# Moving the joined PVs by one round and the score steps by one to six in chunk 0 of a fused attention and SwiGLU block

## The chip, the cores and the metric

The kernel runs on one core of a Trainium2 chip. The metric is the device time of one execution in microseconds (us), the median of several runs. Before the change it is 559.22 us (three runs, 559.13 to 559.57).

## The reference

The block normalises `x` (2048 rows of 576), and adds to `x` a sliding-window attention (32 heads of 18 channels, a window of 256 keys) and a gated SwiGLU network (4608 hidden channels), both of the normalised rows:

```python
xn = layernorm(x)
q, k, v = split_heads(xn @ wqkv)                  # 32 heads, 18 channels
mask = (i - j >= 0) & (i - j < 256)
p = softmax(where(mask, q @ k.T * 18**-0.5, -1e9))
a = (p @ v) @ wo
h = silu(xn @ w1) * (xn @ w3)
out = x + a + h @ w2
```

## The kernel before

The 2048 rows are done in four chunks of 512 (`c` = 0 to 3). A chunk has three stages on TensorE:

- Projections (L449): q, k and v of the chunk's rows. In chunk 0 they stand ahead of everything, with the layer norm.
- Gate and up (`unit_pairs`, L701): 36 **units** `u` of 128 hidden channels. A unit is nine **rounds** `n` = 0 to 8; a round is two matmuls of 64 rows each, one in either half of the array, that run side by side, one into the up bank and one into the gate bank. Behind a unit ScalarE computes a tanh of the gate bank (`unit_tanh`, L710), and VectorE makes `gs` (L716, reads the gate bank) and `hT` (L719, reads the up bank).
- The second product (`p2_list`, L761) with `w2`, 288 matmuls a chunk, and the product with `wo` (L767, L687).

Attention is woven into the gate/up stage of its chunk. Its heads are in eight groups `g` of four; a group has four **score steps** `s` in chunk 0 (32 in all) and five in later chunks (40). A step (g, s) is: scores on TensorE (`scores`, L575), into the two banks kept for them (`SC`, banks 6 and 7), an exp on ScalarE that reads both (`exps`, L584), and masks on POOL (`masks`, L611). The next step's scores must wait until the exp has read the banks. A **PV** `j` (`pv`, L632) multiplies the weights of groups 2j and 2j+1 with v; VectorE takes the result out by two transposes (`pv_out`, L641), then come a reciprocal, a scaling on POOL (`o_scale`, L647), turning (`o_turn`, L654) and DMAs to `oT`. PV 0 stands behind a unit; PVs 1 and 2 stand together, **the joint**, at unit and round `JOINT[c]`; PV 3 stands at the end of gate/up.

PSUM has eight banks. Six make three pairs that are handed out in turn (`job()`): each unit takes a pair, and PV 0 takes one between two units. At the joint, unit u is half done and holds a pair; PV 1 takes the pair of unit u-2 and PV 2 that of unit u-1, so PV 2 must wait until `hT` of unit u-1 is made. The next unit then takes PV 1's pair (so it waits for both of its transposes), and the one behind it PV 2's.

All engines' instructions are written in one order by hand; each engine runs its own in that order, and waits on semaphores are worked out from the buffers (`_Prog`). Where steps stand is set by a planner that counts a clock in rounds: a step may be placed ahead of a round once `clock >= nxt`, a step counts as one round, and

```python
soon = clock + 7.5
room = last - clock - PV_COST * (3 - next_pv) - 5 * sum(v > at_u for v in xt)
nxt = max(soon, clock + room / max(1, len(att) - done))
```

with `last = total - AHEAD[c]`: a smaller `AHEAD` spreads the chunk's steps further towards its end. Steps are at least 7.5 rounds apart, the step itself counted. Ahead of the rounds of a later chunk, steps are also placed among its projections. Weight loads (L322, L349) are issued by SP; some wait for a named round of TensorE.

Of the kernel before, what the change touches and what calls it, by code (L numbers as in the profile page):

```python
# [164 lines left out]
def bass_parallel_sum__sliding_block__glu_gated_swiglu__prompt_kernel(  # L165
# [32 lines left out]
    with ExitStack() as es:  # L198
# [34 lines left out]
        def pt_slot(sl):  # L233
            kind, n = sl
            if kind == "pt":
                return pt[:, n, :, :]
            if kind == "w2":
                return w2[n][:, :, :].rearrange("p f d -> p (f d)")[:, 0:2 * CH].rearrange("p (q r) -> p q r", r=2)
            if kind == "od":
                return od[n][:, :, :].rearrange("p g c -> p (g c)").rearrange("p (q r) -> p q r", r=2)  # L240
            if kind == "sh":
                two = stage[:, 2 * n:2 * n + 2, :]
            else:
                two = hT[:, NF - 8 + 2 * n:NF - 6 + 2 * n, :]
            return two.rearrange("p t c -> p (t c)").rearrange("p (q r) -> p q r", r=2)

        def pt_keys(sl):
            kind, n = sl
            if kind in ("pt", "w2", "od"):
                return [(kind, n)]  # L250
            if kind == "sh":
                return [("sh", 2 * n), ("sh", 2 * n + 1)]
            return [("h", NF - 8 + 2 * n), ("h", NF - 7 + 2 * n)]
# [21 lines left out]
        def job():  # L275
            nonlocal job_ctr
            i = job_ctr % 3
            job_ctr += 1
            return JOBS[i]
# [54 lines left out]
        def owe_part(op):  # L334
            nonlocal owed
            if owed:
                owed -= 1
                load_part((op,))
# [275 lines left out]
        def pv(c, j, banks):  # L614

            seen = set()
            n_all = sum(len(st) for st in steps_of(c))
            n = 0
            for s, st in enumerate(steps_of(c)):
                col = 0  # L620
                for kb, q0, nb in st:
                    n += 1
                    pos = (c * NB + kb) % NV
                    for gi in range(2):
                        g = 2 * j + gi
                        sl = pt_of[(c, g, s)]
                        for pr in range(2):
                            for p in range(2):
                                first = (p, gi, pr) not in seen
                                seen.add((p, gi, pr))  # L630
                                q = 2 * gi + pr
                                add("pe", lambda e, p=p, q=q, pr=pr, sl=sl, g=g, pos=pos, q0=q0, nb=nb, col=col, first=first, n=n: e.matmul(  # L632
                                    PS[32 * q:32 * q + VW, banks[p], q0 * KB:(q0 + nb) * KB],
                                    va[64 * p:64 * p + 64, pos, g, pr, :],
                                    pt_slot(sl)[64 * p:64 * p + 64, col * KB:(col + nb) * KB, pr],
                                    start=first, stop=(n == n_all), tile_position=(64 * p, 32 * q), skip_group_check=True),
                                    r=pt_keys(sl) + [("va", pos)], **{"j" if any(k[0] == p for k in seen - {(p, gi, pr)}) or not first else "w": [("ps", banks[p])]})
                    col += nb

        def pv_out(b, i):  # L640
            add("dve", lambda e, to=uqs[i]: e.transpose(to, PS[:, b, :]), r=[("ps", b)], w=uq_keys[i])  # L641

        def o_scale(i):
            u3 = uqs[i].rearrange("p (n d) -> p n d", d=32)
            o3 = oq[:, :].rearrange("p (n d) -> p n d", d=32)[:, :, 0:Dh]
            add("dve", lambda e: e.reciprocal(rden[:], u3[:, :, Dh]), r=uq_keys[i], w=["rden"])
            add("pool", lambda e: e.tensor_tensor(  # L647
                o3, u3[:, :, 0:Dh], rden[:].unsqueeze(2).to_broadcast([128, CH // 32, Dh]), ALU.mult),
                r=uq_keys[i] + ["rden", "oq0"], w=["oq"])
# [260 lines left out]
        span_main(2, G, "act", slice(0, 2))  # L910

        PV_COST, PV_AFTER = 6.6, 20
        JOINT = {0: (26, 5), 1: (27, 7), 2: (24, 4), 3: (27, 8)}
        AHEAD = [50, 24, 40, 24]

        for c in range(NC):
            NS = len(steps_of(c))
            att = [(g, s) for g in range(G) for s in range(NS)]
            near = {t: tuple(JOINT[c][0] - 13 + 4 * t + k for k in (0, 2, 3)) for t in range(3)} | {3: (34, 35, 40)}
            plan = near if c + 1 < NC else {}  # L920
# [7 lines left out]
            start = 60 if c == 0 else 42  # L928
            last = total - AHEAD[c]
            nxt = soon = start  # L930
            clock = 0.0
            done = 0
            pv_ready = {}
            free = [("pt", n) for n in range(NPT)]
            if c:
                free += [("sh", n) for n in range(4)]
            held = {6 * NS + 1: free.pop(), 6 * NS: free.pop()}
            early = [("h", n) for n in range(4)] + [("w2", (c * 2 * NFC + n) % NW2) for n in range(NW2)]
# [6 lines left out]
            def later(u, what):  # L945
                side.setdefault(u, []).append(what)

            def release(j, kept):
                for g in (2 * j, 2 * j + 1):
                    for st in range(NS):  # L950
                        sl = pt_of[(c, g, st)]
                        ok = ("pt", "sh", "h", "w2") if j == 0 else ("pt", "sh")
                        if sl[0] in ok:
                            (kept if kept is not None and len(kept) < 2 and sl[0] in ("pt", "sh") else free).append(sl)
# [45 lines left out]
            for u in range(NF):  # L1000
# [7 lines left out]
                for n in range(9):  # L1008
                    into = nxt - (clock + 9 - n)
                    if (u, n) == JOINT[c]:  # L1010
                        ja = 1
                        assert next_pv == ja and ja + 1 in pv_ready and clock >= pv_ready[ja + 1], (c, next_pv, clock, pv_ready)
                        two = [job(), job()]
                        job_ctr += 1
                        kept = []
                        _DEBUG.setdefault("joint", []).append((c, u, n, done, round(clock - pv_ready[ja + 1], 1), len([o for o in P.ops if o.eng == "pe"])))
                        for m, j in enumerate((ja, ja + 1)):
                            pv(c, j, two[m])
                            clock += PV_COST
                            release(j, kept)  # L1020
                        next_pv = ja + 2
                        for m, sl in enumerate(kept):
                            uqs[2 + m:] = [pt_slot(sl).rearrange("p q r -> p (q r)").bitcast(dt.float32)]
                            uq_keys[2 + m:] = [pt_keys(sl)]
                        pv_out(two[0][0], 0)
                        pv_out(two[0][1], 1)
                        o_scale(0)
                        pv_out(two[1][0], 2)
                        pv_out(two[1][1], 3)
                        g = 2 * ja  # L1030
                        later(u, lambda g=g: (o_turn(g, 0), o_turn(g, 1), o_scale(1)))
                        later(u + 1, lambda g=g: o_turn(g + 1, 0))
                        later(u + 2, lambda g=g, ja=ja: (o_turn(g + 1, 1), o_pack(ja, "sp"), o_scale(2)))
                        later(u + 3, lambda g=g: (o_turn(g + 2, 0), o_turn(g + 2, 1), o_scale(3)))
                        later(u + 3, lambda kept=kept: free.extend(kept))
                        later(u + 4, lambda g=g: o_turn(g + 3, 0))
                        later(u + 5, lambda g=g, ja=ja: (o_turn(g + 3, 1), o_pack(ja + 1, "sp")))
                    if done < len(att) and (free or done < len(early) or done in held) and (clock >= nxt or (n == 8 and into < 3 and clock >= soon)):
                        spaced_step()
                    op = unit_pairs(c, u, n, n + 1, b0[0])  # L1040
                    clock += 1
                    if n in (3, 8) or (n == 6 and c == 0 and u < 4):
                        owe_part(op)
# [41 lines left out]
                if c == 0 and u == 22:  # L1085
# [3 lines left out]
                    for r in range(2):  # L1089
                        add("sp", lambda e, r=r: e.dma_start(  # L1090
                            wo[64 * r:64 * r + 64, 4, :], head.rearrange("(t d) f -> t d f", d=Dh)[:, 0:16, :]), j=["wo"], dma="wo")
                if u in (range(26, 30) if c == 0 else range(JOINT[c][0], JOINT[c][0] + 7, 2)):
                    load_w2(c * 2 * NFC + 4)
# [68 lines left out]
```

## Time and profile before

| what | value |
|---|---|
| median of three runs | 559.22 us (559.13 to 559.57) |
| the profiled execution | 559.3 us, span 557.6 us |
| TensorE busy | 552.7 us, 99% of the span, 6766 matmuls |
| VectorE, ScalarE, POOL busy | 309.5, 259.5, 163.1 us |
| gate/up (L701), both sources | 183.7 + 151.6 us for the two largest groups |
| second product (L761) | 146.6 us, 1152 matmuls of 286 ns |
| scores (L575) | 51.5 us, 528 matmuls |
| exps (L584), mean by form | about 1010 ns, 1024 wide or a little less |
| tanh, gs, hT, mean | 594, 679, 687 ns |
| mean DMA rate | 154 GB/s |

The span is from the first to the last instruction of the profiled execution; 1.7 us of its time lie outside. In the groups, each matmul has the duration from its start to the modelled end of its pipeline, so two that run side by side or behind each other overlap, and the sum of durations is more than the busy time. A wait is shown as idle time of an engine before an instruction with what released it; gaps of TensorE under 0.15 us are not listed as waits, so a short delay is found from the distance between starts. In the timeline, `[0.34 <-DVE hT L719]` means that the engine was idle for 0.34 us until the instruction of line 719 on VectorE had ended.

The stages by time: opening and projections of chunk 0 to 21.75 us, gate/up of chunk 0 to about 103.2, its second product to 142.9; then chunk 1 to 280.3, chunk 2 to 417.6, chunk 3 to the end.

### The profile page before, as it was taken

The page shows a single profiled execution, that of the slowest core. Times are in us where ns is not written, and L with a number is a line of the kernel's source. Part 1 is how long each engine was busy: PE and PEld are TensorE (multiplying, and loading weights), DVE is VectorE, ACT ScalarE, POOL GpSimd, SP SyncE. Part 2 cuts the span into 40 slices and gives each one's busy share as a digit, 9 for nine tenths or more (in the row PEclk, how much of TensorE's full clock was granted, in tenths as well). Part 3 has the DMA queues.
Part 4 walks back from the last instruction along what each step waited for, and adds up shares of the span by engine and source line. Part 5 has one row for each costly group of instructions (what it writes and reads, how often), then busy time and mean ns, then how long its engine had stood idle before and what let it go on. Part 6 is the DMA issues. An engine that isn't in the chain of part 4 may idle for free.

```text
span 557.6 us, 15733 instructions
## 1 busy us (share of the span) xinstructions
PE 552.7 (99%) x6766; PEld 333.5 (60%) x6766; DVE 309.5 (56%) x578; ACT 259.5 (47%) x357; POOL 163.1 (29%) x389
## 2 busy tenths in 40 slices
PE   8999999999999999999999999999999999999998
PEld 4445454677655445477765544547776554455776
DVE  6476978610356877851045687874105577678211
ACT  6457766100287775700038777640005767755000
POOL 5513644300033452530003445423001333433000
PEclk9999999999999999999999999999999999999999
DMA  9987996877366379566726639685572673734552
GB/s 238 216 167 181 207 186 157 171 197 185 95 139 144 105 177 192 146 168 180 195 65 139 161 106 210 137 201 139 151 187 55 138 173 96 176 107 128 139 149 65
DMA packets 127072, 85.96 MB, mean 154 GB/s; under 512 B 34179, under 2 KB 124763, under 8 KB 127003
## 3 DMA queue, kind: packets, MB, share of 16 engines
q1 hardware_dynamic: 125011, 82.69, 63.0%
q10 hardware_dynamic: 1992, 2.27, 1.8%
q8 instruction: 53, 0.87, 0.7%
q14 instruction: 16, 0.13, 0.1%
HBM read 71.29 MB, written 2.36 MB: 132 GB/s over the span
## 4 chain that ended last, share of the span: by engine, by line
PE 97%; DVE 1%; DMA 1%; ACT 0%; issue 0%; POOL 0%
PE ps L701 50%; PE ps L761 25%; PE ps L449 9%; PE ps L575 6%; PE ps L632 3%; PE ps L767 3%; DMA xp<-in_A_x_dram 1%; PE ps L687 0%; PE ps L394 0%; DVE xn L374 0%; ACT stage L829 0%; ACT xnT L401 0%; DVE hT L719 0%; DVE gs L716 0%; ACT th L710 0%
## 5 line engine op out<-in xcount | busy, mean ns | idle before, releaser
L701 PE MATMUL ps<-xnT,w 64*128 64x512 bf16 x1400 | 183.7, 376 | 0.0
L701 PE MATMUL ps<-xnS,w 64*128 64x512 bf16 x1120 | 151.6, 376 | 0.0
L761 PE MATMUL ps<-w,hT 128*128 128x288 bf16 x1152 | 146.6, 286 | 0.0
L716 DVE SCALAR_TENSOR_TENSOR gs<-th,ps 128x512 bf16<-128x512 bf16 x144 | 97.7, 679 | 78.9 <-ACT th L710 78.5
L761 PEld LDWEIGHTS ps<-w,hT 128*128 128x128 bf16 x1152 | 112.3, 98 | 28.9 <-issue 0.4
L701 PEld LDWEIGHTS ps<-xnT,w 64*128 64x128 bf16 x1400 | 67.1, 94 | 65.7 <-DVE hT L719 0.3
L710 ACT ACTIVATE th<-ps 128x512 bf16<-128x512 f32 x144 | 85.5, 594 | 39.2 <-PE ps L701 37.2
L719 DVE SCALAR_TENSOR_TENSOR hT<-gs,ps 128x512 bf16<-128x512 bf16 x144 | 98.9, 687 | 4.9
L584 ACT ACTIVATE pt<-ps 128x1024 bf16<-128x1024 f32 (+1 forms) x70 | 70.7, 1011 | 39.6 <-PE ps L575 39.5
L701 PEld LDWEIGHTS ps<-xnS,w 64*128 64x128 bf16 x1120 | 53.5, 94 | 51.4
L774 DVE TENSOR_TENSOR ofin<-ps,xp 128x288 bf16<-128x288 f32 x32 | 13.8, 455 | 125.1 <-PE ps L767 67.0
L462 ACT ACTIVATE stage<-ps 128x512 bf16<-128x512 f32 x16 | 9.5, 596 | 142.2 <-PE ps L449 139.8
L611 POOL TENSOR_TENSOR hT<-hT,mk 128x128 int32<-128x128 int32 (+1 forms) x59 | 24.1, 429 | 173.8 <-ACT hT L584 173.7
L611 POOL TENSOR_TENSOR pt<-pt,mk 128x128 int32<-128x128 int32 (+1 forms) x124 | 50.1, 428 | 29.3 <-ACT pt L584 29.1
L575 PE MATMUL ps<-qv,kv 64*128 64x320 bf16 (+4 forms) x528 | 51.5, 260 | 0.0
L575 PEld LDWEIGHTS ps<-qv,kv 64*128 64x128 bf16 x528 | 25.6, 94 | 28.4 <-ACT hT L584 2.3
L449 PE MATMUL ps<-xnT,wp 64*128 64x512 bf16 (+1 forms) x360 | 37.9, 355 | 0.0
L584 ACT ACTIVATE w<-ps 128x1024 bf16<-128x1024 f32 (+1 forms) x32 | 32.3, 1010 | 11.3 <-PE ps L575 11.2
L584 ACT ACTIVATE hT<-ps 128x1024 bf16<-128x1024 f32 (+1 forms) x32 | 32.3, 1009 | 6.6 <-PE ps L575 6.2
L611 POOL TENSOR_TENSOR w<-w,mk 128x128 int32<-128x128 int32 (+1 forms) x56 | 22.8, 427 | 28.2 <-ACT w L584 28.2
L654 DVE STREAM_TRANSPOSE od<-oq 128x256 bf16<-128x256 bf16 x64 | 25.8, 428 | 6.9 <-POOL oq L647 6.9
L449 PEld LDWEIGHTS ps<-xnT,wp 64*128 64x128 bf16 x360 | 18.8, 94 | 14.5 <-POOL wp L885 0.2
(86 smaller groups left out, 380.6 us busy)
## 6 DMA issues: line engine op xcount, KB each, us to landing
w<-in_B_w_dram SPq DMA_DIRECT2D x208, 192.0 KB, 4.0
w<-in_B_w_dram SPq DMA_DIRECT2D x72, 288.0 KB, 3.3
xp<-in_A_x_dram SPq DMA_DIRECT2D x30, 144.0 KB, 3.4
out_dram<-ofin SPq DMA_DIRECT2D x32, 72.0 KB, 1.7
xnS<-xnT SPq DMA_DIRECT2D x8, 256.0 KB, 4.2
oT<-od SPq DMA_DIRECT2D x40, 36.0 KB
pt<-in_A_wqkv_dram SPq DMA_DIRECT2D x4, 288.0 KB, 6.7
hT<-in_B_w_dram SPq DMA_DIRECT2D x6, 192.0 KB, 3.6
```

What stands on the lines that cost most here:

```text
L449: op = add("pe", lambda e, out_=out_, st=st, mv=mv, n=n, r0=r0, first=first: e.matmul(out_, st, mv, start=first, stop=(part == 1 and n == ...
L575: add("pe", lambda e, r0=r0, out_=out_, kb=kb, q0=q0, nb=nb: e.matmul(out_, kb4[r0:r0 + 64, g, kb + NV - NB, :] if kb < 0 else kv[r0:r0 + ...
L584: add("act", lambda e: e.activation(pt_slot(sl)[:, 0:w, :], PS[:, SC[0]:SC[1] + 1, 0:w].rearrange("p r q -> p q r"), ACT.Exp, scale=scale) ...
L611: add("pool", lambda e, vb=vb, mm=mm: e.tensor_tensor(vb, vb, mm, ALU.mult), r=(key if n == 0 else []) + ["mk"], **{"w" if n == 0 else "j" ...
L632: add("pe", lambda e, p=p, q=q, pr=pr, sl=sl, g=g, pos=pos, q0=q0, nb=nb, col=col, first=first, n=n: e.matmul(PS[32 * q:32 * q + VW, banks ...
L654: add("dve", lambda e: e.transpose(od[i][:, g % 2, c0:c0 + CH // 2], oq[:, c0:c0 + CH // 2]), r=["oq", "oq0"], **{"j" if half or g % 2 els ...
L701: op = add("pe", lambda e, n=n, r0=r0, r=r, k=k, src=src: e.matmul(PS[:, b0 + r, :], wt[r0:r0 + 64, k, fl * 128:(fl + 1) * 128], src, star ...
L710: add("act", lambda e: e.activation(th[i][:], PS[:, bg, :], ACT.Tanh, scale=0.5), r=[("ps", bg)], w=[("th", i)])
L716: add("dve", lambda e: e.scalar_tensor_tensor(out=gs[i][:], in0=th[i][:], scalar=1.0, in1=PS[:, bg, :], op0=ALU.add, op1=ALU.mult), r=[("t ...
L719: add("dve", lambda e: e.scalar_tensor_tensor(out=hT[:, u, :], in0=gs[i][:], scalar=0.5, in1=PS[:, bu, :], op0=ALU.mult, op1=ALU.mult), r= ...
L761: add("pe", lambda e: e.matmul(bank, hT[:, f, tt * 128:(tt + 1) * 128], w2[sl][:, k, :], start=(f == 0 and half == 1), stop=False), r=[("h ...
L767: add("pe", lambda e: e.matmul(bank, oT[:, k, tt * 128:(tt + 1) * 128], wo[:, k, d0:d0 + HD], start=False, stop=(k == 3 and (half == 0 or ...
```

## The change

Three lines change. The joint of chunk 0 goes from round 5 to round 6 of unit 26 (the joint is placed ahead of the round). `AHEAD` of chunk 0 goes from 50 to 40. And no step may be placed ahead of round 0 of unit 0 in chunks 1 to 3.

```diff
-        JOINT = {0: (26, 5), 1: (27, 7), 2: (24, 4), 3: (27, 8)}
-        AHEAD = [50, 24, 40, 24]
+        JOINT = {0: (26, 6), 1: (27, 7), 2: (24, 4), 3: (27, 8)}
+        AHEAD = [40, 24, 40, 24]
...
-                    if done < len(att) and (free or done < len(early) or done in held) and (clock >= nxt or (n == 8 and into < 3 and clock >= soon)):
+                    if (c == 0 or u or n) and done < len(att) and (free or done < len(early) or done in held) and (clock >= nxt or (n == 8 and into < 3 and clock >= soon)):
                         spaced_step()
```

What the planner makes of it in chunk 0 (unit/round behind which a step's scores stand):

| step (g, s) | before | after |
|---|---|---|
| (4,2) and all ahead of it | same | same |
| (4,3) | 20/8 | 21/0 |
| (5,0) | 21/6 | 21/7 |
| (5,1) | 22/4 | 22/6 |
| (5,2) | 23/2 | 23/4 |
| (5,3) | 24/0 | 24/2 |
| (6,0) | 24/7 | 25/1 |
| (6,1) | 25/5 | 26/0 |
| joint (PV 1, PV 2), then (6,2) | 26/4 | 26/5 |
| (6,3) | 27/2 | 27/4 |
| (7,0) | 28/0 | 28/3 |
| (7,1) | 28/7 | 29/2 |
| (7,2) | 29/5 | 30/1 |
| (7,3) | 30/3 | 31/0 |

In chunks 1 to 3 every step and PV stands where it stood.

## The prediction

> **What bounds the kernel now.** I read the page's busy lines first, then TensorE's own waits, then the timeline around the two places where the chain of waits breaks. The page:
>
> ```profile
> PE 552.7 (99%) x6766; PEld 333.5 (60%) x6766; DVE 309.5 (56%) x578; ACT 259.5 (47%) x357; POOL 163.1 (29%) x389
> ...
> PEclk9999999999999999999999999999999999999999
> ...
> PE 97%; DVE 1%; DMA 1%; ACT 0%; issue 0%; POOL 0%
> ```
>
> TensorE is busy for 552.7 of 557.6 us, the granted clock is full in every slice, and 97% of the chain is TensorE. Busy need not mean full pace, so I checked the pace: in the chain, 18 gate/up matmuls (nine rounds of two half-array matmuls) take 1.94 us, 0.2156 us a round, and that figure returns in every chunk. A change of order can therefore gain only what TensorE waits. Its waits:
>
> ```profile
> PE ps L796 <- DVE oq L791: 1.2, 1, 1.2
> PE ps L632 <- DVE hT L719: 0.3, 1, 0.3
> PE ps L394 <- DVE xn L374: 0.3, 1, 0.3
> ```
>
> The first and third lie in the opening 22 us, which the change leaves alone. The second is the joined PVs of chunk 0. The timeline there:
>
> ```profile
> 78.27 1.02 ACT L584 ACTIVATE pt<-ps 128x1024 bf16<-128x1024 f32 x1 [0.22 <-PE ps L575]
> 78.48 1.26 PE L701 MATMUL ps<-xnT,w 64*128 64x512 bf16 x10
> ...
> 79.19 0.59 ACT L710 ACTIVATE th<-ps 128x512 bf16<-128x512 f32 x1
> ...
> 79.56 0.40 PE L701 MATMUL ps<-xnS,w 64*128 64x512 bf16 x2
> 79.81 0.69 DVE L716 SCALAR_TENSOR_TENSOR gs<-th,ps 128x512 bf16<-128x512 bf16 x1 [0.32 <-ACT th L710]
> ...
> 79.89 1.05 PE L632 MATMUL ps<-pt,va 64*20 64x320 bf16 x72
> 80.54 0.69 DVE L719 SCALAR_TENSOR_TENSOR hT<-gs,ps 128x512 bf16<-128x512 bf16 x1
> 81.14 0.71 DVE L641 STREAM_TRANSPOSE uq<-ps 128x512 f32<-128x512 f32 x1
> 81.28 0.32 PE L632 MATMUL ps<-hT,va 64*20 64x320 bf16 x4 [0.34 <-DVE hT L719]
> ...
> 81.77 0.68 DVE L641 STREAM_TRANSPOSE ofin<-ps 128x512 f32<-128x512 f32 x1
> ...
> 82.26 0.37 PE L575 MATMUL ps<-qv,kv 64*128 64x320 bf16 x4
> ```
>
> Unit 25's last round starts at 78.48. Its tanh (79.19) stands behind the exp of scores step (6,1), which holds ScalarE from 78.27 to 79.29; gs and hT follow, and hT ends at 81.22. The second PV writes the banks that this hT reads, so it starts at 81.28. The second PV takes 81.28 to 82.26, 0.98 us, and the first has the same shapes; without the wait the second would start at 79.89 + 0.98 = 80.87. **The stall is 0.41 us** (0.34 of it shows as idle, as a matmul's end is modelled).
>
> A second, smaller one shows in no list of waits, only in the pace:
>
> ```profile
> 67.38 0.35 PE L575 MATMUL ps<-qv,kv 64*128 64x320 bf16 x4
> ...
> 67.59 0.60 ACT L710 ACTIVATE th<-ps 128x512 bf16<-128x512 f32 x1 [0.59 <-PE ps L701]
> ...
> 68.18 0.92 ACT L584 ACTIVATE hT<-ps 128x896 bf16<-128x896 f32 x1
> ...
> 68.44 0.81 PE L701 MATMUL ps<-xnS,w 64*128 64x512 bf16 x6
> ...
> 69.24 0.40 PE L575 MATMUL ps<-qv,kv 64*128 64x320 bf16 x4
> ```
>
> Three rounds start at 68.44 and should last 0.647 us, so step (5,0) should start at 69.09; it starts at 69.24. It needs the two score banks that exp (4,3) reads until 69.10, and that exp had stood behind tanh (67.59 to 68.18), because its scores were issued right behind unit 20's last round. **Stall: 0.155 us.** In chunk 0 from here to the chunk's end I find no other gap over 0.04 us that isn't at every PV's head.
>
> **The change, part by part.**
>
> The guard on round 0 of unit 0 in chunks 1 to 3 does nothing: as built, TensorE's order in those chunks is the same to the last instruction (before it, no step stood ahead of that round either). Price 0, from both sides, since no instruction differs.
>
> AHEAD 50 to 40 lets scores of chunk 0 spread over ten more rounds. Thirteen steps move, (4,3) to (7,3), later by 1, 1, 2, 2, 2, 3, 4 rounds ahead of the joint and by 1 (with the joint), 2, 3, 4, 5, 6 behind it. Their exps on ScalarE and masks on POOL move with them; VectorE's and SP's order stay as they were, so no DMA issue changes its place. No instruction is added: 6766 matmuls both times, the steps cost TensorE the same 0.22 us wherever they stand. What can change is waits alone.
>
> Step (4,3) now stands behind round 0 of unit 21 and (5,0) behind round 7. Its exp is still behind tanh (till 68.18), and so still ends at 69.10; step (5,0) arrives one round later, at 69.09 + 0.216 = 69.30, against the 69.24 at which it could start before. It no longer waits: **−0.155**, with 0.06 to spare.
>
> From there I lay the rounds out by the same rows (0.2156 a round, 0.2 a step, a step to its exp 0.43 as in 69.24 to 69.67, exp 1.02 or 0.92). Step (5,2) is the next with only seven rounds since the one ahead: it arrives at 72.93, the banks are free at 72.81. (5,3), (6,0) and (6,1) have more. Step (6,1) now stands behind round 0 of unit 26, so its exp is queued behind tanh of unit 25, no longer ahead of it. Unit 25's round 8 starts about 78.06; tanh starts 0.42 later (67.17 to 67.59 for unit 20), so at 78.5 instead of 79.19; gs and hT take 0.62 + 0.73 + 0.68 more, as before, and hT ends near 80.5.
>
> The joint stands behind round 5 of unit 26 instead of round 4. By these rows the first PV starts at 79.88, the second at 80.86. It needs hT at 80.5 + 0.06. It no longer waits: **−0.41**, with 0.3 to spare. The joint's extra round brings 0.216 of this; the rest is tanh, 0.29 sooner after its round, and the step (0.2) that now lies between that round and the joint. The new place of the step alone would do, the extra round alone would not.
>
> What is late next: round 0 of unit 27 writes the banks of the first PV, and needs both transposes out of them. Cover falls by one round, since three instead of four rounds of unit 26 follow the joint. Chunk 3's joint shows the price of a thinner cover:
>
> ```profile
> 495.39 0.67 DVE L641 STREAM_TRANSPOSE ofin<-ps 128x512 f32<-128x512 f32 x1
> ...
> 496.12 0.65 DVE L641 STREAM_TRANSPOSE pt<-ps 128x512 f32<-128x512 f32 x1
> ```
>
> There only one round follows the joint. The second PV starts at 494.51, the transposes end at 496.07 (1.56 later), and the next unit starts on pace at 496.27, so 0.20 is enough. In chunk 0 after the change: 80.86 + 1.56 = 82.42, and unit 27 starts at 80.86 + 0.98 + 0.2 + 3 × 0.2156 = 82.69: 0.27 to spare. Price 0; if the cover fails, at most the 0.41 is given back (the stall moves).
>
> Behind the joint, steps stand eight rounds apart (1.92 us with the step) against 1.59 for an exp and its hand-over, so none waits. The last, (7,3), goes from 90.84 to about 91.5; PV 3, which needs its masks, stands at 102.18: some 8 us of cover. Weights: those of units 28 to 31 have landed by 78.70 for use at 85.46, those of 32 to 35 by 88.80 for 94.05, so 0.57 less of slack is nothing.
>
> **Sum:** −0.155 − 0.41 = −0.57 us. The profiled execution took 559.3 (span 557.6), which becomes 558.73; the median shown, 559.22, is 0.08 below that execution, which becomes 558.65. All later chunks are TensorE at full pace and pass the gain on.
>
> **The rivals.**
>
> (a) *The scores still wait.* Covers of 0.06 and 0.12 us at (5,0) and (5,2) are thin; if both fail, up to 0.155 comes back: 559.22 − 0.41 = 558.8. For it: the 0.06. Against: both came out positive from measured rows.
>
> (b) *The transposes take the wait's place* at unit 27's first round. Then the 0.41 is given back: 559.22 − 0.155 = 559.06. For it: one round less cover. Against: chunk 3.
>
> (c) *Slower:* tanh of unit 25 still runs behind exp (6,1), whose scores now come later. Place: ScalarE, about 79. The exp would run 78.9 to 79.9, hT would end near 81.95, the second PV would stall for 82.0 − 80.86 = 1.14 us in place of 0.41: −0.155 + 0.73 = +0.57, 559.8. It decides from a tanh that starts later than 78.77 on (2.03 to the end of hT, 0.06 to the PV at 80.86), and breaks even at 79.34. Against it: the built order has tanh first, and its input is ready 0.45 us sooner.
>
> (d) *Faster by more:* TensorE may run slow for a while after a wait, so that the stall costs more than its length. At the kernel's start matmuls of 512 columns follow each other at 0.427 us, half rate; were 3.4 us of rounds behind the joint at half rate, their cure would give 1.7 more, 557.0. Against it: behind the stall rounds start at 82.46, 82.68, 82.89, 83.11, 83.33, at 0.217.
> The Trainium skill ("TensorE: Matmul & The Clock Gate", "What's actually happening") says the array falls to half rate only after an idle window of about 3.4 us. By that rule the 0.41 us stall cannot trip it and (d) gives nothing; the rounds just quoted agree.
>
> **How the numbers follow.** Forecast 0.75 (558.65); (a) 0.10; (b) 0.08; (c) 0.04; (d) 0.02; 0.01 for what I do not see. A measurement of this kernel tells about 0.2%, 1.1 us, from no change, so the forecast, (a), (b) and (c) all count as no change: 0.94; faster 0.03, which is (d) and half of the unseen; slower 0.03, which is (c) with a second stall behind it. The range takes in the forecast, (a) and (b), and the spread of the runs (−0.09 to +0.35 about their median): 558.2 to 559.3.
>
> **What would show it.** Right: TensorE's list of waits has no L632 behind hT; the second PV starts 0.98 after the first; tanh of unit 25 starts before exp (6,1); step (5,0) comes 0.65 after the last three rounds; chunk 1's first unit starts 0.57 earlier, and chunks 1 to 3 last as long as before. Wrong: an L701 row waiting for L641 near 82.5 (b), an L575 row late behind L584 (a), or a difference that arises in a later chunk, where I hold that nothing changed.

## The result and the profile after

The changed kernel takes 558.68 us (median of 22 runs, 558.42 to 560.84), the kernel before, on the same chips, 559.60 (22 runs, 559.08 to 562.02). The ratio of the two times is 0.9983, 95% interval 0.9976 to 0.9990: 0.17% faster, within the 0.2% that counts as no change here, though the interval leaves 1 out. Forecast were 558.7 and a gain of 0.57; the three later comparisons of the same two kernels gave gains of 0.70, 1.01 and 0.61 us.

The profiled execution (`after` below) took 558.67 us, with a span of 557.0. Two lines of its page, the busy times and the chain's shares by engine:

```profile
PE 552.4 (99%) x6766; PEld 342.6 (62%) x6766; DVE 310.1 (56%) x578; ACT 259.7 (47%) x357; POOL 163.0 (29%) x389
...
PE 98%; DMA 1%; DVE 0%; ACT 0%; issue 0%; POOL 0%
```

The page hardly differs from that of before; a change of 0.1% isn't read from shares. TensorE's list of waits does differ:

```profile
PE ps L796 <- DVE oq L791: 1.2, 1, 1.2
PE ps L394 <- DVE xn L374: 0.3, 1, 0.3
```

The line for L632 behind hT is gone. The timeline of the changed kernel around the joint (start, duration, engine, line):

```profile
78.31 0.60 PE L701 MATMUL ps<-xnT,w 64*128 64x512 bf16 x4
78.73 0.60 ACT L710 ACTIVATE th<-ps 128x512 bf16<-128x512 f32 x1 [0.49 <-PE ps L701]
78.74 0.38 PE L575 MATMUL ps<-qv,kv 64*128 64x320 bf16 x6
...
79.23 1.02 ACT L584 ACTIVATE pt<-ps 128x1024 bf16<-128x1024 f32 x1
...
80.08 0.69 DVE L719 SCALAR_TENSOR_TENSOR hT<-gs,ps 128x512 bf16<-128x512 bf16 x1
80.14 1.05 PE L632 MATMUL ps<-pt,va 64*20 64x320 bf16 x72
81.00 0.31 PE L632 MATMUL ps<-hT,va 64*20 64x320 bf16 x4
...
81.25 0.72 DVE L641 STREAM_TRANSPOSE uq<-ps 128x512 f32<-128x512 f32 x1 [0.48 <-PE ps L632]
...
81.89 0.67 DVE L641 STREAM_TRANSPOSE ofin<-ps 128x512 f32<-128x512 f32 x1
81.98 0.37 PE L575 MATMUL ps<-qv,kv 64*128 64x320 bf16 x4
```

Unit 25's round 8 starts at 78.31, its tanh at 78.73, now ahead of exp (6,1) at 79.23. hT ends at 80.77, 0.23 ahead of the second PV at 81.00, which follows the first by 0.86 us (before: 81.28 - 79.89 = 1.39). Around step (5,0), the same view:

```profile
67.79 0.60 ACT L710 ACTIVATE th<-ps 128x512 bf16<-128x512 f32 x1 [0.59 <-PE ps L701]
...
67.80 0.36 PE L575 MATMUL ps<-qv,kv 64*128 64x320 bf16 x4
...
68.37 0.92 ACT L584 ACTIVATE hT<-ps 128x896 bf16<-128x896 f32 x1
...
68.64 1.03 PE L701 MATMUL ps<-xnS,w 64*128 64x512 bf16 x8
...
69.50 0.38 PE L575 MATMUL ps<-qv,kv 64*128 64x320 bf16 x4
```

Four rounds from 68.64 end at 69.50, where (5,0) starts: no wait, though the exp that it needs is behind tanh as before and ends at 69.29.

Where the time went is read best between marks behind the opening, whose length differs by some tenths from execution to execution. From the first matmul of unit 14 in chunk 0 to that of unit 0 in chunk 1:

| execution (us) | unit 14 to chunk 1 | first to second PV | round ahead of (5,0) | chunk 1 | chunk 2 |
|---|---|---|---|---|---|
| before | 104.23 | 1.389 | 0.372 | 137.39 | 137.28 |
| after | 103.48 | 0.859 | 0.2156 | 137.37 | 137.30 |
| after, three more | 103.52, 103.49, 103.50 | 0.860, 0.861, 0.860 | the same | 137.41, 137.44, 137.28 | 137.31, 137.25, 137.28 |

Here 0.71 to 0.75 us go, all of it in this stretch of chunk 0: 0.53 at the joint, 0.155 at step (5,0), the rest too small to be put down. Chunks 1 and 2 agree with those of before to 0.11. The kernel before was traced once, so 104.23 and 1.389 are single readings; the runs below test them.

### The profile page after: what moved, and what is told of

It is laid out like the page before. It is cut to its first block, busy times and chain, and to the rows that moved or that the text cites. A ratio compares the mean times of both kernels' runs of the same rounds, so it can differ in the third digit from the quotient of the medians.

```text
span 557.0 us, 15733 instructions
## 1 busy us (share of the span) xinstructions
PE 552.4 (99%) x6766; PEld 342.6 (62%) x6766; DVE 310.1 (56%) x578; ACT 259.7 (47%) x357; POOL 163.0 (29%) x389
## 4 chain that ended last, share of the span: by engine, by line
PE 98%; DMA 1%; DVE 0%; ACT 0%; issue 0%; POOL 0%
PE ps L701 50%; PE ps L761 25%; PE ps L449 9%; PE ps L575 6%; PE ps L632 3%; PE ps L767 3%; DMA xp<-in_A_x_dram 1%; PE ps L687 0%; PE ps L394 0%; DVE xn L374 0%; ACT stage L829 0%; ACT xnT L401 0%; DVE stats L357 0%; DVE ofin L774 0%; POOL xn L377 0%
## 5 line engine op out<-in xcount | busy, mean ns | idle before, releaser
L701 PEld LDWEIGHTS ps<-xnT,w 64*128 64x128 bf16 x1400 | 71.6, 94 | 61.1
L701 PEld LDWEIGHTS ps<-xnS,w 64*128 64x128 bf16 x1120 | 57.4, 94 | 48.1
```

The costliest lines, as they stand in the source:

```text
L701: op = add("pe", lambda e, n=n, r0=r0, r=r, k=k, src=src: e.matmul(PS[:, b0 + r, :], wt[r0:r0 + 64, k, fl * 128:(fl + 1) * 128], src, star ...
```

## The experiments

Each comparison is with the kernel before on the same chip: medians, their ratio and its 95% interval, which is about ±0.5 us. So the medians tell the large differences only; the stalls are read from the traces. In the four of the changed kernel the distance between the PVs repeats to 0.002 us, and the whole stretch to 0.04. Two times given as "A against B" are the run and the kernel before.

**The changed kernel again** (`e0_after_again`, `e8_after_beside`, `e11_after_third`), to compare on the chips of the others.

> The changed kernel again, on the chip that the next two run on. Theory: -0.69 us against before (0.53 at the joint, 0.155 at step (5,0)). Rival (my sum on record, with the joint's stall at 0.41): -0.57.

558.95 against 559.65, ratio 0.9993 (0.9984 to 1.0002).

> The changed kernel beside it. Theory: -0.69 us against before; first to second PV 0.86, unit 14 of chunk 0 to unit 0 of chunk 1 in 103.5 us.

558.79 against 559.80, ratio 0.9979 (0.9970 to 0.9987); 0.861 and 103.49 as expected.

> The changed kernel beside the two, for a comparison on one chip: -0.7 us against before.

558.78 against 559.39, ratio 0.9985 (0.9976 to 0.9994). The traces are in the table above. The medians can't tell -0.57 from -0.69; the traces can, and their -0.71 to -0.75 is nearer to the latter.

**The joint alone** (`e1_joint_only`)

```diff
-        AHEAD = [40, 24, 40, 24]
+        AHEAD = [50, 24, 40, 24]
```

> Joint at unit 26 round 6, pace of before (AHEAD 50). Theory (two stalls, 0.53 us at the joint by the trace of after, 0.155 at step (5,0); the extra round is worth one round and the new place of the tanh the rest): the joint's stall falls by one round, 0.216, to about 0.31, step (5,0) still waits; -0.22 us against before, 559.4 if before is 559.6. TensorE's waits still name L632 behind hT L719. Rival (the later joint by itself cures its stall): no such wait, -0.53.

559.11 against 559.62, ratio 0.9991 (0.9982 to 1.0000). The median lies on the rival's side, the trace doesn't. Its timeline:

```profile
78.36 1.02 ACT L584 ACTIVATE pt<-ps 128x1024 bf16<-128x1024 f32 x1 [0.22 <-PE ps L575]
...
79.28 0.59 ACT L710 ACTIVATE th<-ps 128x512 bf16<-128x512 f32 x1
...
80.20 1.05 PE L632 MATMUL ps<-pt,va 64*20 64x320 bf16 x72
80.63 0.69 DVE L719 SCALAR_TENSOR_TENSOR hT<-gs,ps 128x512 bf16<-128x512 bf16 x1
...
81.37 0.32 PE L632 MATMUL ps<-hT,va 64*20 64x320 bf16 x4
```

The exp is again ahead of tanh, hT ends at 81.32, and the second PV starts 1.174 behind the first: 0.314 of stall, against 0.53 before. One round is worth one round. The stall is still there, but the idle time shown of it is under the 0.15 us from which TensorE's list names a wait, since matmuls' modelled ends cover the first part; the expected line in that list was wrong. Step (5,0) waits as before (the round ahead of it takes 0.363, before 0.372). From unit 14 to chunk 1 it takes 104.03, 0.20 less than before.

**The pace alone** (`e2_pace_only`)

```diff
-        JOINT = {0: (26, 6), 1: (27, 7), 2: (24, 4), 3: (27, 8)}
+        JOINT = {0: (26, 5), 1: (27, 7), 2: (24, 4), 3: (27, 8)}
```

> Joint at unit 26 round 5 as before, pace of after (AHEAD 40). Theory: step (5,0) no longer waits (-0.155), tanh of unit 25 runs ahead of exp (6,1) and step (6,1) lies between, so the joint's stall falls from 0.53 to about 0.05: -0.64 against before. Rival (the joint's round does the work, the pace only cures the score step): the stall of about 0.5 stays, -0.155.

559.00 against 559.62, ratio 0.9988 (0.9979 to 0.9997).

```profile
78.63 0.60 ACT L710 ACTIVATE th<-ps 128x512 bf16<-128x512 f32 x1 [0.49 <-PE ps L701]
...
79.81 1.05 PE L632 MATMUL ps<-pt,va 64*20 64x320 bf16 x72
79.98 0.69 DVE L719 SCALAR_TENSOR_TENSOR hT<-gs,ps 128x512 bf16<-128x512 bf16 x1
80.72 0.32 PE L632 MATMUL ps<-hT,va 64*20 64x320 bf16 x4
...
81.10 0.47 PE L632 MATMUL ps<-hT,va 64*20 64x128 bf16 x4
81.35 0.23 PE L632 MATMUL ps<-w,va 64*20 64x128 bf16 x4
```

The second PV starts 0.906 behind the first: 0.047 of stall is left, as worked out, and (5,0) doesn't wait. So the pace does nearly all of it, and the joint's round the rest. (Within this PV there is a pause of 0.24 us, 81.10 to 81.35, with no waiting shown; more on such pauses below. Without it the stretch, 103.79, would be 0.68 shorter than before.)

**The joint two rounds sooner** (`e4_joint_26_3`, an edit of the kernel before)

```diff
-        JOINT = {0: (26, 5), 1: (27, 7), 2: (24, 4), 3: (27, 8)}
+        JOINT = {0: (26, 3), 1: (27, 7), 2: (24, 4), 3: (27, 8)}
```

> The kernel before with the joint two rounds sooner, at round 3. Theory (the second PV waits for hT of unit 25, which is fixed by unit 25's last round): the stall grows by two rounds, 0.43, to about 0.96, +0.43 against before. Rival (the stall belongs to the joint itself and not to its distance from unit 25, or cover behind the joint gains what is lost): no change against before.

559.89 against 559.62, ratio 1.0006 (0.9998 to 1.0015); from unit 14 to chunk 1 104.60, 0.37 more than before.

```profile
79.86 1.05 PE L632 MATMUL ps<-pt,va 64*20 64x320 bf16 x72
...
81.59 0.32 PE L632 MATMUL ps<-hT,va 64*20 64x320 bf16 x4 [0.68 <-DVE hT L719]
```

First to second PV 1.73, so 0.87 of stall, and the round ahead of the first PV is 0.09 longer than before (0.416 against 0.326), as the first now waits for unit 24's hT. Together 0.96, as expected, 0.43 more than before: the stall follows the joint's distance from unit 25. (The whole stretch grew by 0.06 less than that. In this trace step (5,0) waited 0.025 less and PV 3 took 0.037 less than in the one of before.)

**The joint one and two rounds later** (`e6_joint_26_7`, `e3_joint_26_8`)

```diff
-        JOINT = {0: (26, 6), 1: (27, 7), 2: (24, 4), 3: (27, 8)}
+        JOINT = {0: (26, 7), 1: (27, 7), 2: (24, 4), 3: (27, 8)}
```

This is the edit of the first; the second has 8 in place of 7.

> The kernel after with the joint one round later, at round 7. Theory (both transposes out of the first PV's banks must end ahead of unit 27; they end 1.56 us behind the second PV's start, and in after have 0.27 to spare): 0.05 left, no change against after, -0.69 against before, at most 0.02 of wait. Rival (a later joint is always better or the cover is already used up in after): faster than after, or slower by a whole round, 0.2.

558.68 against 559.62, ratio 0.9985 (0.9976 to 0.9994). The second transpose out of the first PV's banks:

```profile
81.83 0.67 DVE L641 STREAM_TRANSPOSE ofin<-ps 128x512 f32<-128x512 f32 x1
```

It ends at 82.50. The first matmul of unit 27 starts at 82.52, the one beside it, in the other half of the array, 0.05 later; in after both start together. Up to unit 32 nothing is lost (41.22 from unit 14, as in after), but the whole stretch to chunk 1 takes 103.56, against 103.48 to 103.52. So the cover is just used up: about 0.05 of wait where at most 0.02 was expected. The next run shows where such a lag is paid.

> The kernel after with the joint at round 8, one round ahead of unit 27. Theory: the transposes (L641) end two rounds later than in after, near 83.0 on its scale, and unit 27 wants to start at 82.83; with 0.06 of hand-over it waits 0.2 us: +0.2 against after, -0.47 against before. Rival (the cover does not matter, as in chunk 3, where one round was enough): same as after.

559.07 against 559.65, ratio 0.9992 (0.9983 to 1.0001). The transposes of the kernel with the joint at round 8:

```profile
81.60 0.72 DVE L641 STREAM_TRANSPOSE uq<-ps 128x512 f32<-128x512 f32 x1 [0.95 <-PE ps L632]
82.24 0.67 DVE L641 STREAM_TRANSPOSE ofin<-ps 128x512 f32<-128x512 f32 x1
```

The second one ends at 82.91, and unit 27 was due at 82.75. But it isn't late as a whole. Of the two matmuls of a round, the first writes the bank that came free at 82.32 and starts on time at 82.75, the second starts at 82.97, and from there both halves run at full pace, one 0.22 behind the other, for all of units 27 to 35 (unit 35's first round: 99.32 and 99.53; in after 99.38 and 99.38). The price comes at PV 3, at the chunk's end. TensorE there, first with the joint at round 8:

```profile
101.05 0.59 PE L701 MATMUL ps<-xnT,w 64*128 64x512 bf16 x2
101.27 0.62 PE L687 MATMUL ps<-wo,oT 64*128 64x288 bf16 x4
101.83 1.05 PE L632 MATMUL ps<-pt,va 64*20 64x320 bf16 x72
```

and in after:

```profile
101.11 0.38 PE L701 MATMUL ps<-xnT,w 64*128 64x512 bf16 x2
101.32 0.41 PE L687 MATMUL ps<-wo,oT 64*128 64x288 bf16 x4
101.68 1.05 PE L632 MATMUL ps<-pt,va 64*20 64x320 bf16 x72
```

From unit 35's last round to PV 3 it is 0.78 against 0.57. The whole, unit 14 to chunk 1, is 103.75, 0.25 more than after. The theory had the size (0.2) and not the place; no list of waits shows any of it. At round 7 the lag is 0.05, and it is paid at the same place: from the last but one matmul of L687 to PV 3 it takes 0.276 against 0.233.

**The guard one round further** (`e5_guard2`, `e7_guard2_again`)

The guard as it stands forbids a place that no step took. The step that does wait, in chunks 1 and 2, stands one round behind. TensorE in the changed kernel at the start of chunk 1:

```profile
155.82 0.38 PE L701 MATMUL ps<-xnT,w 64*128 64x512 bf16 x2
156.19 0.31 PE L575 MATMUL ps<-qv,kv 64*128 64x320 bf16 x2
```

0.37 instead of 0.2156 for the one round: 0.15 of wait. (Chunk 2 shows 0.38.)

The edit of both runs (the rest of the line is left out):

```diff
-                    if (c == 0 or u or n) and done < len(att) ...
+                    if (c == 0 or u or n > 1) and done < len(att) ...
```

> The kernel after with the guard reaching one round further: in chunks 1 to 3 no step stands ahead of round 1 of unit 0 either. In chunks 1 and 2 step (0,2) then stands behind round 1 in place of round 0, where it waits 0.165 us for exp (0,1) in both traces. Theory: both waits go, -0.33 against after, -1.0 against before. Rival (the wait only moves to step (0,3), whose banks come free just in time, since ScalarE's v copies hold exp (0,2) up): same as after.

559.43 against 559.65, ratio 1.0000 (0.9988 to 1.0012): the theory's total is off by 0.8. By stages it holds in part: chunk 1 takes 137.16 (after 137.28 to 137.44) and chunk 2 137.09 (137.25 to 137.31), and neither start shows the wait:

```profile
156.92 0.61 PE L701 MATMUL ps<-xnT,w 64*128 64x512 bf16 x4
157.35 0.32 PE L575 MATMUL ps<-qv,kv 64*128 64x320 bf16 x2
```

Two rounds in 0.43. But chunk 0 lost 0.8, though its gate/up has the instructions of after: 0.48 ahead of unit 16, where the last weight load landed 5.1 us after its issue instead of 3.5, and a pause of 0.28 within the second PV.

> The kernel with the guard one round further, a second time, beside the changed kernel on one chip: in its first profile chunks 1 and 2 were each 0.2 us shorter, while chunk 0, whose instructions are those of the changed kernel, was 0.8 longer in that one execution (a weight transfer at unit 16, a pause within the second PV). Theory: the 0.2 each in chunks 1 and 2 comes again, and chunk 0 does not repeat its loss: -0.33 to -0.4 against the changed kernel. Rival (the guard's shift of steps costs chunk 0 something after all): chunk 0 is again 0.5 us or more longer.

559.64 against 559.80, ratio 0.9991 (0.9983 to 1.0000). Chunk 2 took 137.08, again 0.2 less. Chunk 0 lost 0.6 ahead of unit 16 again (the same load landed after 5.2 us), and chunk 1 1.5 in one pause in the middle of a round of unit 9. So the theory holds for chunk 2, and its other half fails: chunk 0 did lose 0.6 again, which was the rival's sign. The edit acts only from chunk 1 on, and `e9` below, with the same guard but row loads issued otherwise, has no such loss in chunk 0. Still, the late load (`e5`, `e7`) and the pause at unit 9 (`e7`, `e9`) were seen in traces with this guard alone, and in none of the other eleven. Whether the guard brings them on or they fell on it by chance is not shown.

**Row loads moved to ScalarE** (`e9_x_on_act_guard2`, with the guard one round further; `e10_x_on_act`, without), to give that weight load more room.

```diff
-                loads[6] = (0, 1)
+                loads = {4: (0, 1), 5: (2,), 17: (3,)}
...
-                        xslot[(c + 1) * TB + i] = load_x((c + 1) * TB + i)
+                        xslot[(c + 1) * TB + i] = load_x((c + 1) * TB + i, "act" if c == 0 and u < 6 else "sp")
```

> The guard one round further, and chunk 1's first three row loads (L298) issued by ScalarE at units 4 and 5 in place of SP at units 6 and 8. In the traces the last weight load of units 16 to 19 (L322) is issued by SP at 51.2 to 52.2, behind those row loads at 49.1, and lands 0.1 to 1.2 us ahead of unit 16; in both profiles of the guard alone it landed late and unit 16 started 0.5 us late. Theory: SP gains 2 us there, the load lands 2 to 3 us ahead, unit 16 never waits; the runs lose their upper half, median 558.3, -0.4 against the changed kernel. Rival (the upper half of the runs has another source, or ScalarE's issues delay exps): the runs spread as before.

560.40 against 559.39, ratio 1.0009 (0.9998 to 1.0021). The load was issued at 51.5 and landed 1.6 us ahead of unit 16; in the four traces of the changed kernel it was 0.9 to 1.5 us, and 2 to 3 were expected. Chunk 0 was whole (103.55) and chunk 2 again short (137.10), but chunk 1 paused once more at the same place of unit 9:

```profile
178.16 0.81 PE L701 MATMUL ps<-xnS,w 64*128 64x512 bf16 x5
180.23 0.60 PE L701 MATMUL ps<-xnS,w 64*128 64x512 bf16 x3 [1.26 <-issue]
```

"issue" says that TensorE waited for nothing that the profile shows. Beside it: on a queue that the profile's page calls instruction, blocks of 16 KB come in, 53 in the whole execution. The block that lies ahead of the pause starts at 177.3 here and at 178.1 in the other paused execution, and at 174.5 to 175.9 in the twelve without the pause (among them the first of the guard). That these blocks are TensorE's instructions, and that a late one is the cause, is likely, not shown.

> The changed kernel with the row loads on ScalarE alone, no other edit. Theory: as above without the 0.4 of the guard; same lowest runs as the changed kernel (558.4 to 558.5), fewer above 559. Rival: no change of the spread.

559.43 against 559.39, ratio 0.9995 (0.9986 to 1.0004). The load was again issued at 51.95 and landed 0.4 us ahead: SP had the key moves (L545) where the row loads had been, and then waited for TensorE's round as before. So SP gained nothing, and the theory of the spread fell: ten of the twelve runs lie above 559, against three of twelve of the changed kernel on the same chip. The edit may cost something; its one trace is of the fastest run (558.30) and doesn't show what. No version here beats the changed kernel by its median; the joint at round 7 equals it.

## Why the prediction was right, point by point

- **The guard is void.** Right: chunks 1 and 2 last as before to 0.11 us, and their first round still waits.
- **Step (5,0): -0.155.** Right in size and place. The thin cover (0.06 worked out) held in all four traces of the changed kernel. The pace alone cures it, the joint alone doesn't.
- **The joint: -0.41.** Right in kind, 0.12 too small. The failed step is "the second PV takes 81.28 to 82.26, 0.98 us, and the first has the same shapes", and with it the sign "the second PV starts 0.98 after the first". Without a wait the first takes 0.86 to the next one's start, and the second, which is followed by scores, 0.98 to 1.02 (1.23 and 1.27 in the two traces with a pause in it). The difference is at the end: from a PV's last matmul to the first score it is 0.15, to the first matmul of the next PV 0.02 to 0.03. (A PV's matmuls use 20 columns of the array, the scores 128; that this is the reason is likely, not shown.) So the stall was 1.389 - 0.859 = 0.53, which `e1`, `e2` and `e4` confirm (0.31, 0.05 and 0.96, as worked out with 0.53). The forecast with it would have been -0.69 and 558.5.
- **Why it goes.** "The new place of the step alone would do, the extra round alone would not": with the larger stall the pace leaves 0.047, the round 0.314. Nearly right; both are needed for zero.
- **The late transposes (b).** 1.57 behind the second PV's start (1.56 worked out), unit 27 1.83 behind it (1.83): 0.26 of cover. One round less is just too much, by 0.05 (`e6`). (a), (c) and (d) did not come about: none of the moved score steps waits, tanh of unit 25 is ahead of the exp by 0.5 us, and the gain (0.71 to 0.75) is hardly more than the two stalls (0.69).
- **The sum.** -0.57 against -0.71 to -0.75 by the traces and -0.61 to -1.01 by the medians. That the forecast time, 558.7, met the measured 558.68 is in part luck: the three runs of before that it started from (559.22) lay lower than the 22 (559.60), which made up for a gain put too small. From 559.60 the same sum gives 559.03.

## What to carry to other kernels

When one engine is busy for 99% of the span, look for its waits by the distance between starts against the known pace: of the two stalls that this change removed, one stood in no list, and the other stood there with 0.34 of its 0.53 us. Place score work so that its exp is queued behind the tanh whose result someone waits for, not ahead of it. And measure a step's length from a place with the same successor: a PV's 72 matmuls took 0.86 or 0.98 depending on what followed.

## What the runs showed of the hardware

- Two matmul streams in the two halves of the array can run 0.22 us apart for 18 us without loss (`e3`); there the lag of one half is paid (0.21 us) only at the next PV. In `e7` and `e9` the pause at unit 9 left a lag of 0.21, later 0.17, that ran on to the joint of chunk 1 at unit 27, some 40 us behind it; there the round ahead of the first PV took 0.48 instead of 0.31.
- From the last matmul of a gate/up round to the first of a PV, 0.305 to 0.307 us pass, in every chunk and every trace but `e4`, where the PV waits. From a PV's last matmul to what follows, scores or the second product, it is 0.146 to 0.152 in chunk 0 and 0.202 to 0.213 later; to the next PV it is 0.02 to 0.03 in chunk 0, where nothing waits, and 0.01 to 0.07 later.
- The same weight load, of 192 KB, landed 3.5 to 5.2 us after its issue from run to run. The one that unit 16 needs landed 0.4 to 2.7 us ahead of the unit in twelve traces and was late in two (the guard one round further, `e5` and `e7`), which cost 0.5 to 0.6 us there.
